# Turning gathered rows by transposing transfers in a routed mixture of experts

## The chip, the cores and the metric

One core of a Trainium2 chip runs the whole program. The metric is device time in microseconds (us) of one execution; the lower the better. TensorE (PE) multiplies matrices, VectorE (DVE) and ScalarE (ACT) work element by element, GpSimd (POOL) and SyncE (SP) mostly issue transfers (DMAs), each from a queue of its own and in program order.

## The reference, cut to what matters

A chunked attention gives rows `x` of 3072 x 512; a noisy router picks two of eight experts for each row; each expert is two products with a relu between them.

```python
N, D, E, F = (3072, 512, 8, 1024)
logits = x @ w_gate
noise_scale = np.log1p(np.exp(x @ w_noise))
noisy_logits = logits + noise_scale * noise
top2 = np.argpartition(-noisy_logits, 2, axis=1)[:, :2]
...
for e in range(E):
    for k in range(2):
        mask = top2[:, k] == e
        ...
        h = np.maximum(x[mask] @ w1[e], 0.0)
        out[mask] += top2_w[mask, k, None] * (h @ w2[e])
```

## The kernel before, in words

**Two stages.** Up to about 114 us the kernel computes the attention and the routing, and writes the rows (512 values in bf16, packed as 256 32-bit words, and eight gates) to a tensor `x_rows` in DRAM. The rest is the experts, and the change lies there.

**Buckets.** A row has two experts, so it belongs to one of 28 pairs of experts, the buckets, numbered `p`. A bucket holds up to 128 rows; what overflows goes through a small spill path. Each expert works on seven buckets, and each bucket is worked on by two experts. So expert 0 meets seven new buckets, expert 1 six, expert 2 five, and so on down to one for expert 6 and none for expert 7. `plan[e]` lists the new ones of expert `e`. `halves(e)` gives its seven buckets as a larger half of four and a smaller of three. For experts 1 and 2 the larger half is all new (expert 1: buckets 1, 9, 17, 25; the smaller half is 0, 15, 22, of which 0 is shared with expert 0); for expert 3 the new ones are exactly the larger half; from expert 4 on the larger half has been met before and the new ones are in the smaller.

**One bucket's way.** `gather(p)` (L696, GpSimd) fetches 128 rows by an indirect transfer into a tile `xl`, of which there are eight in turn. `turn(p)` needs the rows the other way round, since a product contracts over partitions: four transposes on TensorE (L705) of 128 x 128 into PSUM tile `p_t`, one copy by VectorE (L706) from there into `xTb`, which holds all 28 buckets and is never overwritten, and a copy of the gates into `meta` by ScalarE (L707). `first` (L769) multiplies `xTb` by the expert's first weights `w1t` into `ps_h`, eight blocks of the hidden width one after the other, the larger half and then the smaller; the relu (L754, L756) writes `ht`. `second` (L780) multiplies a bucket of `ht` by `w2t` into `ps_y`. The first expert of a bucket puts the result, scaled by the gate, in `acc` (L784); the second adds its own (L787), and then GpSimd scatters the bucket to the output (L788) and, for most buckets, SyncE copies its last six rows to `spart` (L795), which is read in the last expert only.

**The order.** It is written out by hand and kept on each engine. Expert 0 is special: three parts with their turns in between, a search for the spilled rows, and `turn_spill`, which makes SyncE issue six small copies to `meta` (L730). For every expert: `first`, then the gathers for the next expert (in two cases later in time, as a buffer or an index comes free), a load of weights, then the seven second products, and behind each of them one turn for the next expert:

```python
            for j, p in enumerate(order):
                second(e, p, ht, j, W2[e])
                if nxt:
                    turn(nxt.pop(0))
```

Where a tile is written by one engine or transfer and read by another, the framework puts in a wait on a semaphore. The transfers of SyncE use eight semaphores in turn, and each transfer waits until the one that used its semaphore before it has landed.

Of the kernel before, what the change touches and what calls it, by code (L numbers as in the profile page):

```python
# [12 lines left out]
F32 = mybir.dt.float32  # L13
BF16 = mybir.dt.bfloat16
# [10 lines left out]
def kernel(  # L25
# [14 lines left out]
    nc = tc.nc  # L40
# [8 lines left out]
    KP = Dm // 128  # L49
# [19 lines left out]
    XC = Dm // 2  # L69
# [29 lines left out]
    def body():  # L99
# [63 lines left out]
        for hd in range(2 * GP):  # L163
            nc.sync.dma_start(
                out=mv_nat[QW * hd + WP:QW * hd + QW].rearrange("p g e d -> p g (e d)"),
                in_=bass.AP(mem_v.tensor, mem_v.offset + hd * n_mem * D, [[2 * D, n_mem // 2], [2 * GP * n_mem * D, NG], [1, 2 * D]]))
# [518 lines left out]
        xTv = xTb.rearrange("p k (g c) -> p k g c", c=CAP)  # L685
        meta = xg.tile([128, NB, E], F32, name="meta")
# [13 lines left out]

        def turn(p, other=False):
            xl = got[p]
            p_t = psY.tile([128, KP, CAP], BF16, name="p_t2", tag="ps_y") if other else psX.tile([128, KP, CAP], BF16, name="p_t")
            for kp in range(KP):
                nc.tensor.transpose(out=p_t[:, kp, :], in_=xl[:, kp * 64:(kp + 1) * 64].bitcast(BF16), identity=identb)  # L705
            nc.vector.tensor_copy(xTv[:, :, p, :], p_t)  # L706
            nc.scalar.copy(meta[:, p, :], xl[:, XC:].bitcast(F32))  # L707
# [90 lines left out]
        plan = []  # L798
# [78 lines left out]
        for e in range(E):  # L877
# [6 lines left out]
            if e == 0:  # L884
                parts = [big[:2], big[2:], small]
                off = 0
                for x, ps in enumerate(parts):
                    for j, p in enumerate(ps):
                        turn(p, j % 2 == 1)
                    if x == 2:  # L890
                        turn_spill()
                        find_tails()
                    first(W1[e], ht, off, ps, nc.scalar if x == 0 else None, CAP if x == 2 else OWN, big if x == 2 else ())
                    off += len(ps)
                    if x == 0:
                        s_gi, s_si = find_spill()
                        gather_spill(s_gi)
                        load_w2(1)
            else:
                first(W1[e], ht, 0, big)  # L900
                first(W1[e], ht, len(big), small)
# [7 lines left out]
# [4 lines that stand above are left out]
                if e == E - 1 and j == 1:  # L913
                    for x in range(1, E // 2 - 1):
                        nc.vector.tensor_tensor(out=spart[:, 0, :], in0=spart[:, 0, :], in1=spart[:, x, :], op=Alu.add)
            if e == E - 1:
# [3 lines left out]
                    out=out_part[NB], out_offset=bass.IndirectOffsetOnAxis(ap=s_si[:, 0:1], axis=0),  # L920
                    in_=spart[:, 0, :], in_offset=None, bounds_check=N - 1, oob_is_err=False)
            while nxt:
                turn(nxt.pop(0))
# [9 lines left out]
    with tc.For_i(SPILL, end, 128) as i:  # L933
# [7 lines left out]
        for t in range(NP):  # L941
# [9 lines left out]
        xl = ld.tile([128, ROW], I32, name="xl")  # L951
        nc.gpsimd.indirect_dma_start(
            out=xl, out_offset=None, in_=xd, in_offset=bass.IndirectOffsetOnAxis(ap=gi[:, 0:1], axis=0),
# [10 lines left out]
        with tc.For_i(0, E, 1) as e:  # L964
# [17 lines left out]
            out=out, out_offset=bass.IndirectOffsetOnAxis(ap=si[:, 0:1], axis=0),  # L982
            in_=o, in_offset=None, bounds_check=N - 1, oob_is_err=False)
# [30 lines left out]
```

## Time and profile before

| | |
|---|---|
| median of 3 runs | 334.02 us (332.93 to 334.89) |
| the profiled execution | 335.33 us, span from first to last instruction 333.7 us |
| busy: TensorE, VectorE, ScalarE, GpSimd | 288.1, 169.9, 133.4, 138.6 us |
| mean granted TensorE clock | 0.957 of full speed |
| DMA packets | 58763, 42.99 MB |
| the turns: L705 on TensorE, L706 on VectorE | 112 transposes, 28 copies |

How to read it: times are microseconds from the span's start. A row of the timeline gives start, length, engine, line and the tiles as written<-read, and in brackets how long the engine sat idle before it and what ended that. Matmuls overlap in the pipeline, so the start of the next group says more about a group's cost than its own length. Rows with SPq are the queue in which SyncE issues transfers; their times are the issue and not the transfer.

### The profile page before, as it was taken

Reading aid. Unit: us, or ns where it says so; the run is one execution under the profiler, and the core shown is the slowest. Engines: PE = TensorE matmul, PEld = TensorE weight load, DVE = VectorE, ACT = ScalarE, POOL = GpSimd, SP = SyncE. Lnnn points to the kernel's source line nnn. Section 1 sums busy time; section 2 is a strip of 40 time slices with the busy share of each in tenths; the row PEclk is TensorE's granted clock in tenths of the full one; section 3 lists DMA queues with packets and bytes.
Section 4 is the critical chain, followed back from the end, with each engine's and each line's share of the span. In section 5 each row is a group of like instructions: output and inputs, shape, how many; then the busy total and the mean of one; then the engine's idle time right before and its main releaser. Section 6 shows DMA issues by size and latency. Waiting matters only on the chain.

```text
span 333.7 us, 7301 instructions
## 1 busy us (share of the span) xinstructions
PE 288.1 (86%) x3019; PEld 173.5 (52%) x3019; DVE 169.9 (51%) x343; ACT 133.4 (40%) x235; POOL 138.6 (42%) x181
## 2 busy tenths in 40 slices
PE   1697887977776377999999999999999999999990
PEld 0575675755654256554754754544544544544540
DVE  7789859849958775222322323424342433434451
ACT  7877788757433033533333332332303303202200
POOL 7877868538023472781008007007152042042152
PEclk9999999979989559999999999999999999999997
DMA  7999999999997136699407905914959624521031
GB/s 99 179 163 176 184 163 163 210 143 101 214 225 216 23 88 93 128 156 238 87 0 125 221 4 110 223 28 105 207 147 166 117 111 70 86 109 60 1 140 71
DMA packets 58763, 42.99 MB, mean 129 GB/s; under 512 B 32449, under 2 KB 52033, under 8 KB 58728
## 3 DMA queue, kind: packets, MB, share of 16 engines
q0 software_dynamic: 49808, 38.71, 77.0%
q1 hardware_dynamic: 8632, 3.74, 5.6%
q8 instruction: 24, 0.39, 0.5%
q10 hardware_dynamic: 288, 0.07, 0.1%
q14 instruction: 11, 0.09, 0.1%
HBM read 61.23 MB, written 10.66 MB: 215 GB/s over the span
## 4 chain that ended last, share of the span: by engine, by line
PE 43%; issue 24%; DVE 13%; ACT 8%; POOL 7%; DMA 3%; POOLq 0%; DVEq 0%; ACTq 0%
PE ps_h L769 16%; PE ps_y L780 14%; POOL out_dram L788 4%; ACT kd L276 3%; PE ps_o L345 3%; DMA out_dram<-acc,sidx 2%; PE ps_o L341 2%; DVE mx L313 2%; DVE xrow L358 2%; DVE sd L318 2%; DVE vg L150 2%; PE p_t L705 2%; ACT xt L371 1%; ACT P L320 1%; PE p_t L265 1%
## 5 line engine op out<-in xcount | busy, mean ns | idle before, releaser
L769 PE MATMUL ps_h<-xTb,w1t 128*128 128x512 bf16 (+5 forms) x640 | 101.4, 320 | 1.5 <-DVE xTb L706 1.5
L780 PE MATMUL ps_y<-w2t,ht 128*128 128x512 bf16 x448 | 101.4, 379 | 0.0
L769 PEld LDWEIGHTS <-w1t 128*128 128x128 bf16 x640 | 58.6, 99 | 43.9 <-DVE xTb L706 1.1
L788 POOL DMA_INDIRECT out_dram<-acc,sidx x28 | 28.1, 1004 | 126.4 <-DVE acc L787 124.1
L756 DVE TENSOR_SCALAR ht<-ps_h 128x512 bf16<-128x512 f32 (+3 forms) x68 | 38.1, 560 | 68.1 <-PE ps_h L769 63.1
L780 PEld LDWEIGHTS <-ht 128*128 128x128 bf16 x448 | 42.9, 98 | 46.7
L754 ACT ACTIVATE ht<-ps_h 128x384 bf16<-128x384 f32 (+2 forms) x76 | 38.9, 511 | 70.4 <-PE ps_h L769 66.3
L784 ACT ACTIVATE acc<-ps_y,meta 128x512 f32<-128x512 f32 x28 | 19.2, 687 | 62.6 <-PE ps_y L780 45.4
L787 DVE SCALAR_TENSOR_TENSOR acc<-ps_y,meta,acc 128x512 f32<-128x512 f32 x28 | 21.0, 750 | 34.5 <-PE ps_y L780 34.5
L696 POOL DMA_INDIRECT xl<-x_rows,gidx x28 | 30.0, 1071 | 16.8 <-PE ps_h L769 6.6
L134 POOL DMA_DIRECT2D vg<-in_v_dram x34 | 25.5, 756 | 11.4 <-DMA kg<-in_k_dram 3.7
L706 DVE COPY xTb<-p_t 128x512 bf16<-128x512 bf16 x28 | 11.6, 422 | 28.6 <-PE p_t L705 28.4
L276 ACT COPY kd<-p_t 64x768 bf16<-64x768 bf16 x32 | 25.2, 786 | 1.0 <-PE p_t L265 0.8
L265 PE MATMUL p_t<-identb,qg 128*64 128x128 bf16 x192 | 10.3, 245 | 12.0 <-DMA qg<-in_q_dram 6.6
L371 ACT COPY xt<-p_x 128x768 bf16<-128x768 bf16 x16 | 12.8, 798 | 12.0 <-PE p_x L369 11.9
L341 PE MATMUL ps_o<-memv,PT 128*128 128x260 bf16 x96 | 15.0, 296 | 2.2 <-DVE PT L332 2.0
L320 ACT ACTIVATE P<-sd 128x768 bf16<-128x768 f32 x16 | 13.5, 845 | 8.1 <-DVE sd L318 8.1
L268 ACT COPY qT<-p_t 128x768 bf16<-128x768 bf16 x16 | 12.8, 800 | 8.9 <-PE p_t L265 8.8
L358 DVE TENSOR_TENSOR xrow<-ps_o,rec 128x768 bf16<-128x768 f32 x16 | 15.3, 958 | 0.6
L313 DVE TENSOR_REDUCE mx<-ps_s 128x12 f32<-128x768 f32 x16 | 15.1, 942 | 0.5 <-PE ps_s L300 0.5
L318 DVE TENSOR_TENSOR sd<-ps_s,mx 128x768 f32<-128x768 f32 x16 | 15.2, 949 | 0.0
L345 PE MATMUL ps_o<-vg,PT 128*32 128x256 bf16 x384 | 14.9, 293 | 0.0
(150 smaller groups left out, 287.5 us busy)
## 6 DMA issues: line engine op xcount, KB each, us to landing
w1t<-in_moe_w_dram POOLq DMA_DIRECT2D x8, 1024.0 KB, 11.4
w2t<-in_moe_w_dram POOLq DMA_DIRECT2D x8, 1024.0 KB, 10.1
vg<-in_v_dram POOLq DMA_DIRECT2D x30, 168.0 KB, 10.2
qg<-in_q_dram POOLq DMA_DIRECT2D x7, 384.0 KB, 9.9
kg<-in_k_dram POOLq DMA_DIRECT2D x7, 384.0 KB, 11.3
x_rows<-xrow SPq DMA_DIRECT2D x3, 792.0 KB
x_rows<-xrow SPq DMA_DIRECT2D x2, 384.0 KB
xl<-x_rows,gidx POOLq DMA_INDIRECT x28, 6.5
```

The lines of the kernel that those rows point to most:

```text
L134: nc.gpsimd.dma_start(out=vg[p0 + j:p0 + j + nj, c:c + n, hd, :, :].rearrange("p c e d -> p c (e d)"), in_=bass.AP(v.tensor, v.offset + (g ...
L276: nc.scalar.copy(st[n]["kT"][hs, hh, :].rearrange("d (p j) -> d p j", j=SJ), st[n]["p_k"][hs].rearrange("d j p -> d p j"))
L313: nc.vector.tensor_reduce(out=mx, in_=st[n]["ps"], axis=AX, op=Alu.max)
L318: nc.vector.tensor_tensor(out=sd, in0=st[n]["ps"], in1=bc4(st[n]["mx"], CTX), op=Alu.subtract)
L345: nc.tensor.matmul(out=po[32 * r:32 * r + 32, u, :MD], lhsT=PT[:, 2 * u + e, 32 * r:32 * r + 32], rhs=vg[:, CB * half + x, :, e, :], start ...
L358: nc.vector.tensor_tensor(out=xr.rearrange("p u (h d) -> p u h d", d=D), in0=po[:, :, :MD].rearrange("p u (h d) -> p u h d", d=D), in1=rec ...
L696: nc.gpsimd.indirect_dma_start(out=xl, out_offset=None, in_=xd, in_offset=bass.IndirectOffsetOnAxis(ap=idx[:, p:p + 1], axis=0), bounds_ch ...
L754: nc.scalar.activation(out=dst, in_=src, func=Act.Relu)
L756: nc.vector.tensor_scalar(out=dst, in0=src, scalar1=0.0, scalar2=None, op0=Alu.max)
L769: nc.tensor.matmul(out=ps_h[:, o:o + w], lhsT=w1t[:, kp, f * 128:(f + 1) * 128], rhs=rhs(kp), start=(kp == 0 and i == 0), stop=(kp == KP - ...
L780: nc.tensor.matmul(out=ps_y, lhsT=ht[:, f, j * CAP:(j + 1) * CAP], rhs=w2t[:, f, :], start=(f == 0), stop=(f == FB - 1))
L788: nc.gpsimd.indirect_dma_start(out=out_part[p], out_offset=bass.IndirectOffsetOnAxis(ap=sidx[:, p:p + 1], axis=0), in_=a, in_offset=None, ...
```

## The change

For the buckets that expert 0 doesn't meet (21 of the 28), `turn` issues four transposing transfers on SyncE's queue, from `xl` straight into `xTb`, both in SBUF. The transposes of TensorE, the PSUM tile and VectorE's copy are left out for them; ScalarE's copy of the gates stays. Expert 0's seven buckets and the spilled rows are turned as before. The calls of `turn` stand where they stood.

```diff
         def turn(p, other=False):
             xl = got[p]
+            if p not in plan[0]:
+                for kp in range(KP):
+                    nc.sync.dma_start_transpose(out=xTv[:, kp, p, :], in_=xl[:, kp * 64:(kp + 1) * 64].bitcast(BF16))
+                nc.scalar.copy(meta[:, p, :], xl[:, XC:].bitcast(F32))
+                return
             p_t = psY.tile([128, KP, CAP], BF16, name="p_t2", tag="ps_y") if other else psX.tile([128, KP, CAP], BF16, name="p_t")
             for kp in range(KP):
                 nc.tensor.transpose(out=p_t[:, kp, :], in_=xl[:, kp * 64:(kp + 1) * 64].bitcast(BF16), identity=identb)
```

SyncE's order before, from the last write of `x_rows` on; the copies to `spart` are named by the buffer of `acc` that they read:

```order
L548 DMA x_rows<-xrow 128x6x8
L730 DMA meta<-xl 6x8 x6
L795 DMA spart<-acc_2650 6x512
L795 DMA spart<-acc_2657 6x512
L795 DMA spart<-acc_2651 6x512
L795 DMA spart<-acc_2663 6x512
L795 DMA spart<-acc_2658 6x512
```

And the same place now (lines below the change have moved by five):

```order
L548 DMA x_rows<-xrow 128x6x8
L735 DMA meta<-xl 6x8 x6
L705 DMA_TRANSPOSE xTb<-xl 128x128 x40
L800 DMA spart<-acc_2650 6x512
L705 DMA_TRANSPOSE xTb<-xl 128x128 x20
L800 DMA spart<-acc_2657 6x512
L800 DMA spart<-acc_2651 6x512
L705 DMA_TRANSPOSE xTb<-xl 128x128 x12
L800 DMA spart<-acc_2663 6x512
L800 DMA spart<-acc_2658 6x512
L800 DMA spart<-acc_2652 6x512
```

The first 40 are the 24 of expert 1 and 16 of expert 2's 20; the copies to `spart` now stand between transfers. With what each waits for (DMASW is a gather or another transfer of GpSimd, DMAHW one of SyncE's eight semaphores), the first nine read:

```order
L705 DMA_TRANSPOSE xTb<-xl 128x128 [waits DMASW3_49,DMASW2_49,DMASW7_49,DMASW1_49,DMAHW2_49,DMASW0_49,PE_49]
L705 DMA_TRANSPOSE xTb<-xl 128x128 [waits DMAHW3_49]
L705 DMA_TRANSPOSE xTb<-xl 128x128 [waits DMAHW4_49]
L705 DMA_TRANSPOSE xTb<-xl 128x128 [waits DMAHW5_49]
L705 DMA_TRANSPOSE xTb<-xl 128x128 [waits DMAHW6_49,DMASW1_49]
L705 DMA_TRANSPOSE xTb<-xl 128x128 [waits DMAHW7_49]
L705 DMA_TRANSPOSE xTb<-xl 128x128 [waits DMAHW0_49]
L705 DMA_TRANSPOSE xTb<-xl 128x128 [waits DMAHW1_49]
L705 DMA_TRANSPOSE xTb<-xl 128x128 [waits DMAHW2_49,DMASW2_49]
```

Before, nothing of this stood in SyncE's queue; now a bucket's first transfer waits for its gather, and every transfer for the one eight places ahead.

TensorE's order between the first two second products of expert 0, before:

```order
L780 LDWEIGHTS ht
L780 MATMUL ps_y<-w2t_164,ht 128x512
L705 LDWEIGHTS xl
L705 MATMUL p_t<-identb,xl 128x128
L705 LDWEIGHTS xl
L705 MATMUL p_t<-identb,xl 128x128
L705 LDWEIGHTS xl
L705 MATMUL p_t<-identb,xl 128x128
L705 LDWEIGHTS xl
L705 MATMUL p_t<-identb,xl 128x128
L780 LDWEIGHTS ht
L780 MATMUL ps_y<-w2t_164,ht 128x512
```

And now:

```order
L785 LDWEIGHTS ht
L785 MATMUL ps_y<-w2t_164,ht 128x512
L785 LDWEIGHTS ht
L785 MATMUL ps_y<-w2t_164,ht 128x512
L785 LDWEIGHTS ht
```

The four transposes of the turn are gone, and the products follow each other.

## The prediction

> **What bounds the kernel now.** I read the page first (busy time, the forty slices), then the chain that ended last, then a table by stretches and the waits of TensorE.
>
> The engines' busy time and two rows of the forty slices (8.34 us each):
>
> ```profile
> PE 288.1 (86%) x3019; PEld 173.5 (52%) x3019; DVE 169.9 (51%) x343; ACT 133.4 (40%) x235; POOL 138.6 (42%) x181
> ...
> PE   1697887977776377999999999999999999999990
> ...
> PEclk9999999979989559999999999999999999999997
> ```
>
> From slice 16 on (133 us) TensorE is full to the end, at full granted clock. The change lies wholly in that stretch, so TensorE's order is what it must shorten, and anything that makes TensorE wait there costs its whole length. The chain in order of time (start, length, what), from the second halves of expert 0 on; L769 is a first product (`first`), L780 a second (`second`):
>
> ```profile
> 150.83 1.73 PE ps_y L780 x8
> 152.55 12.19 PE ps_h L769 x96
> 164.74 1.73 PE ps_y L780 x8
> 166.69 1.73 PE ps_y L780 x8
> ...
> 177.94 12.19 PE ps_h L769 x96
> 190.13 1.73 PE ps_y L780 x8
> ...
> 203.11 12.11 PE ps_h L769 x64
> 215.22 1.73 PE ps_y L780 x8
> ...
> 227.97 2.60 PE ps_h L769 x12
> ```
>
> An expert takes some 25 us: 12.2 for the first product, seven second products of 1.73. Between 130 and 320 us these are TensorE's only waits, 0.9 us in all (total, times, longest):
>
> ```profile
> PE p_t L720 <- DVE xTb L706: 0.5, 1, 0.5
> PE p_t L705 <- DVE xTb L706: 0.4, 1, 0.4
> ```
>
> **What is removed.** Behind a second product that has a turn the next one starts 1.95 us later (166.69 less 164.74) and not 1.73: a turn's four transposes cost TensorE 0.22 us. The changed code leaves out 21 turns, 6 beside expert 0's second products, then 5, 4, 3, 2 and 1: 21 x 0.22 = **4.6 us**, all on the path. VectorE's copy goes too, and is worth nothing by itself:
>
> ```profile
> L706 DVE COPY xTb<-p_t 128x512 bf16<-128x512 bf16 x28 | 11.6, 422 | 28.6 <-PE p_t L705 28.4
> ```
>
> It waits for TensorE 28.6 us, never the other way in these stages except for the 0.9 above, which belong to expert 0 and stay. ScalarE's copy of the gates stays.
>
> **What is added.** SyncE issues 84 transposing transfers, four a bucket, in one queue: 24 for expert 1, 20, 16, 12, 8, 4. No such transfer stands in this trace. Nearest rows: what SyncE's transfers hold it for now (ns, min/median/max), and the gathers on GpSimd, whose starts lie 1.32 to 1.38 us apart:
>
> ```profile
> L548 SPq DMA_DIRECT2D x_rows<-xrow x6: 359/362/371, 58.8 to 111.2; - x6
> L795 SPq DMA_DIRECT2D spart<-acc x24: 663/670/743, 175.2 to 324.5; - x24
> 134.27 1.07 POOL L696 DMA_INDIRECT xl<-x_rows,gidx  x1 [6.03 <-PE ps_h L769]
> 135.65 1.02 POOL L696 DMA_INDIRECT xl<-x_rows,gidx  x1 [0.31 <-PE ps_h L769]
> 136.97 1.01 POOL L696 DMA_INDIRECT xl<-x_rows,gidx  x1 [0.30 <-PE ps_h L769]
> xl<-x_rows,gidx POOLq DMA_INDIRECT x8, 2.9
> xl<-x_rows,gidx POOLq DMA_INDIRECT x5, 10.2
> ```
>
> The last two rows are gathers' times from issue to landing, in 134 to 146 us and in 144 to 156 us, where two or three weight loads are under way. So the pace of one transfer is between 0.36 us (a plain copy of SyncE) and, as an outer bound, 2.9 us (if each held the queue until it landed). I take **1.32 us**, the gather's pace: a gather too is one instruction made into many small pieces, 128 rows of it, while SyncE's copies are few long runs. There is a second reason for a figure there: the transfers use eight semaphores in turn, and each waits for the one eight places ahead. At a landing of 2.9 us that bounds the pace at 0.36, but at 10.2 us at 1.28. I take 2.9 us from a transfer's start to its landing.
>
> [...]
>
> **The sum.** SyncE can start when expert 1's first gather has landed: 134.27 + 2.9 = 137.2. Transfer n has landed at 137.2 + 1.32(n-1) + 2.9. A first product needs its larger half (four buckets) before it begins, the other half after 4/7 of it (12.19 x 4/7 = 7.0; the rest 5.2).
>
> Expert 1. TensorE is ready at 152.55 - 6 x 0.22 = 151.2. Transfer 16 lands at 159.9: a **wait of 8.7**. After a pause TensorE's clock is lower. These rows show it (granted clock is the third figure from the right; then the chain's rows for two equal sets of 32 matmuls):
>
> ```profile
> 115.00:119.80 4.80, 1.22 (x8) 0.80 (x9) 1.61 (x10) 0.40 (x2) 3.58 (x5) 0.50 0.32 85
> 119.80:125.40 5.60, 5.59 (x33) 4.14 (x33) 5.12 (x4) 2.58 (x7) 3.83 (x3) 0.60 0.32 89
> 125.40:130.60 5.20, 4.26 (x47) 3.81 (x47) 2.56 (x11) 2.12 (x10) 1.99 (x2) 1.00 0.38 40
> 119.81 5.63 PE ps_h L769 x32
> 127.07 3.52 PE ps_h L769 x32
> ```
>
> The set behind a stretch with little work took 5.63 us at 0.60, the other 3.52: 2.1 us lost, which I add once, for this wait. Half one ends at 159.9 + 7.0 + 2.1 = 169.0. Transfer 24 lands at 170.5 (wait 1.5), half two ends at 175.7, 11.0 later than the 164.74 of the chain.
>
> Expert 2. Second products 12.1, to 187.8. Transfer 40 lands at 191.6 (**wait 3.8**); the last bucket's four stand behind one copy to spart (0.67) and land at 197.6, in time for 198.6. The first product ends at 203.8, the second products at 215.9.
>
> Expert 3. Its gathers stand on GpSimd behind the scatter of expert 1's shared bucket and a weight load:
>
> ```profile
> 174.37 0.75 DVE L787 SCALAR_TENSOR_TENSOR acc<-ps_y,meta,acc 128x512 f32<-128x512 f32 x1 [1.37 <-PE ps_y L780]
> 175.41 1.04 POOL L788 DMA_INDIRECT out_dram<-acc,sidx  x1 [24.14 <-DVE acc L787]
> 176.43 0.96 POOL L543 DMA_DIRECT2D w2t<-in_moe_w_dram  x1
> 177.70 1.08 POOL L696 DMA_INDIRECT xl<-x_rows,gidx  x1 [0.30 <-issue]
> w2t<-in_moe_w_dram POOLq DMA_DIRECT2D x8, 1024.0 KB, 10.1
> ```
>
> That bucket is the fifth second product: 175.7 + 5 x 1.73 + 0.75 + 1.04, and the gathers land after the load of 10.1: 196.2. SyncE is free just before (137.2 + 44 x 1.32 + 0.7 = 196.0). Sixteen transfers: 196.2 + 15 x 1.32 + 2.9 = 218.9 against 215.9, **wait 3.0**. One more expert (12.1 + 12.1) brings the first product of expert 4 to 243.1 where it was at 227.97: 15.1 later.
>
> From there the new halves come second and are covered. Expert 4's gathers land behind expert 2's sixth second product, two scatters and a load (203.8 + 6 x 1.73 + 0.75 + 2 x 1.04 + 10.1 = 227.1), their twelve transfers at 227.1 + 11 x 1.32 + 2.9 = 244.5, wanted at 243.1 + 7.0 = 250. Expert 5's eight stand behind copies that wait for expert 4's second products, and land about 3 us before they are wanted. Three turns left save 0.7. Together 15.1 - 0.7 = **14.4 us later**: waits of 8.7 + 1.5 + 3.8 + 3.0 and 2.1 of clock, less 4.6.
>
> Nothing else comes late. Expert 2's last three gathers wait until transfers 4, 8 and 12 have freed their buffers (154.6 for the last), and behind them on GpSimd stands a load of expert 3's weights:
>
> ```profile
> 150.43 0.84 POOL L538 DMA_DIRECT2D w1t<-in_moe_w_dram  x1
> ```
>
> It goes from 150.4 to about 156 and is wanted at 219. The copies to spart that wait in SyncE's queue are read only in the last expert.
>
> The profiled execution took 335.33 us (span 333.7), 1.3 above the median of 334.02. On it the sum gives 349.7, on the median **348.4 us**.
>
> **Rivals.** A change of 0.5% (1.7 us) is about what a measurement of this kernel tells from none. By the same walk a pace of 0.93 us gives 333, no change; that is the point that decides. A pace of 1.8 gives waits that add up to 42.7 us net, 377.
>
> 1. *A cheap transfer.* SyncE issues a transposing transfer like its other copies, 0.36 to 0.67 us. At 0.67 transfer 16 lands at 150.2, ahead of 151.2; no later one waits, and the 4.6 us are won: **329.4**, faster. For it: SyncE's own rows and its queue, idle all this time. Against it: none of its rows turns anything, and the dearer ones carry only 6 rows. Chance 0.13. [...]
>
> 2. *One at a time.* If the queue is held until a transfer has landed, the pace is 2.9: sixty transfers end at 137.2 + 174 = 311 where expert 3 began at 203.1, and with waits at experts 4 and 5 the kernel takes about **454**. For it: no transposing transfer stands in the trace, so nothing there excludes it. Against it: SyncE's copies and GpSimd's gathers leave their queues long before they land. Chance 0.05.
>
> 3. *A tie*, a pace near 0.9: waits of about 4 us take back the 4.6. Within 0.5%. Chance 0.04.
>
> **How the numbers follow.** My forecast, a pace from 0.95 to 1.8 with 1.32 likeliest, has the remaining 0.78, all of it slower. So slower 0.78 + 0.05 = 0.83, same 0.04, faster 0.13. The range runs from the tie, 333, to 378, a pace of 1.8; it leaves out rival 1, rival 2 and 0.02 between, 0.20 in all.
>
> **What would show it.** Right: SyncE's rows of L705 pitched at 1.2 to 1.4 us; TensorE's wait at L769's start for expert 1 about 9 us on xTb's transfers, two more of 3 to 4 us at experts 2 and 3, none at 5 to 7; a low clock in one slice near 160 us; second products 1.73 apart without gaps. Wrong: a pitch under 0.95 and no such waits (rival 1), a pitch that grows with the weight loads to over 1.8, waits at experts 4 to 6 too, or transfers that land long after 2.9 us, so that the last, not the pace, decides.

## The result, and the profile after

The changed kernel took 355.37 us (median of 4 runs, 350.13 to 357.6) beside 334.05 for the kernel before: a ratio of 1.0547 (95% interval 1.0426 to 1.0669), slower. Here and below a ratio is that of undisturbed runs of both kernels on one chip, so it can differ a little from the quotient of two medians. The profiled execution took 354.41 us, span 352.8, against 335.33 and 333.7: 19.1 us more span, where the sum said 14.4.

The page of the changed kernel: busy time, the slices (8.82 us each), and SyncE's DMA queue (packets, MB, share):

```profile
PE 288.5 (82%) x2935; PEld 169.9 (48%) x2935; DVE 161.2 (46%) x322; ACT 133.4 (38%) x235; POOL 138.6 (39%) x181
...
PE   1797887878773679919694899999999899999990
...
PEclk9999998989996599987999699999999999999996
...
q1 hardware_dynamic: 22072, 6.50, 9.9%
```

TensorE has 84 matmuls fewer and is as long busy as before; its mean granted clock has fallen from 0.957 to 0.938. Its row is full from 133 us on no longer: slices 17 (a tenth), 19 and 21 (counted from 0) have holes, and slices 18 and 22, behind the holes, the low clock (digits 7 and 6). Before, SyncE's queue had moved 8632 packets:

```profile
q1 hardware_dynamic: 8632, 3.74, 5.6%
```

SyncE's transfers in the changed kernel (ns, min/median/max; then its queue's timeline: start, length, count), and two steps of the chain:

```profile
L705 SPq DMA_TRANSPOSE xTb<-xl x84: 1093/1230/2133, 137.2 to 290.6; - x84
137.23 53.43 SPq L705 DMA_TRANSPOSE xTb<-xl  x40
190.76 0.73 SPq L800 DMA_DIRECT2D spart<-acc  x1
191.59 26.84 SPq L705 DMA_TRANSPOSE xTb<-xl  x20
138.51 1.21 SPq L705
139.77 1.23 SPq L705
```

A transfer holds the queue for 1.23 us and the next starts 0.05 later (139.77 less 138.51 is 1.26, 138.51 less 137.23 is 1.28), for 53 us on end. From the first start to that of the fortieth (189.18, below) it is 1.33 a transfer. Each bucket takes SyncE more than 5 us; TensorE needed 0.22.

TensorE's wait for it between 130 and 352 us (total, times, longest), and its timeline at experts 1, 2, 3, 5 and 7 (in brackets the idle time and its releaser):

```profile
PE ps_h L774 <- DMA xTb<-xl: 18.4, 6, 8.1
159.37 8.59 PE L774 MATMUL ps_h<-xTb,w1t 128*128 128x512 bf16 x33 [8.14 <-DMA xTb<-xl]
170.71 5.45 PE L774 MATMUL ps_h<-xTb,w1t 128*128 128x256 bf16 x63 [2.74 <-DMA xTb<-xl]
175.99 12.25 PE L785 MATMUL ps_y<-w2t,ht 128*128 128x512 bf16 x56
188.08 0.38 PE L774 MATMUL ps_h<-xTb,w1t 128*128 128x512 bf16 x1
191.55 0.39 PE L774 MATMUL ps_h<-xTb,w1t 128*128 128x512 bf16 x1 [3.09 <-DMA xTb<-xl]
194.92 0.59 PE L774 MATMUL ps_h<-xTb,w1t 128*128 128x512 bf16 x1 [2.98 <-DMA xTb<-xl]
195.83 13.71 PE L774 MATMUL ps_h<-xTb,w1t 128*128 128x512 bf16 x93 [0.32 <-DMA xTb<-xl]
209.37 12.25 PE L785 MATMUL ps_y<-w2t,ht 128*128 128x512 bf16 x56
221.46 12.27 PE L774 MATMUL ps_h<-xTb,w1t 128*128 128x512 bf16 x64
278.64 4.87 PE L774 MATMUL ps_h<-xTb,w1t 128*128 128x384 bf16 x29 [1.12 <-DMA xTb<-xl]
319.63 12.27 PE L774 MATMUL ps_h<-xTb,w1t 128*128 128x512 bf16 x64
```

The same places in the kernel before, in the same view:

```profile
152.39 12.35 PE L769 MATMUL ps_h<-xTb,w1t 128*128 128x512 bf16 x96
177.78 12.35 PE L769 MATMUL ps_h<-xTb,w1t 128*128 128x512 bf16 x96
202.95 12.27 PE L769 MATMUL ps_h<-xTb,w1t 128*128 128x512 bf16 x64
301.06 12.27 PE L769 MATMUL ps_h<-xTb,w1t 128*128 128x512 bf16 x64
```

With these rows the difference closes. Up to expert 3's first product (221.46 less 202.95 = 18.5 later) there are waits of 8.14 + 2.74 at expert 1 and 3.09 + 2.98 + 0.32 at expert 2, 17.3 in all. First products took 12.19 before; expert 1's now takes 175.99 - 159.37 - 2.74 = 13.9, expert 2's 209.37 - 188.08 - 6.39 = 14.9, which adds 4.4. Fifteen turns left out are worth 15 x 0.22 = 3.3. So 17.3 + 4.4 - 3.3 = 18.4. From there to expert 7 (319.63 less 301.06 = 18.6) six more turns save 1.3, a wait of 1.12 at expert 5 and some 0.3 in its pipeline take that back, and 0.5 is lost behind the last expert.

The clock in these stretches (last three figures: granted clock, DMA share, GB/s):

```profile
159.40:168.00 8.60, 8.56 (x33) 3.46 (x33) 2.13 (x4) 2.39 (x4) 1.84 (x2) 0.83 0.81 131
188.00:196.00 8.00, 1.61 (x6) 0.32 (x4) 0.00 (x0) 0.69 (x1) 4.97 (x5) 0.82 1.06 162
196.00:209.50 13.50, 13.50 (x94) 8.21 (x93) 4.44 (x7) 4.35 (x8) 0.00 (x0) 0.85 0.73 142
```

Over the two stretches behind a wait, the first row and the third, the clock averaged 0.83 and 0.85. And why expert 2's transfers landed late: the fortieth in the chain, and the load that GpSimd had issued just before:

```profile
189.18 6.60 DMA xTb<-xl
186.96 0.96 POOL L543 DMA_DIRECT2D w2t<-in_moe_w_dram  x1
```

The transfer that started at 189.18 landed 6.6 us later, at 195.78, not 2.9 later. The two ahead of it, started some 2.6 and 1.3 us earlier, were waited for until 191.55 and 194.92, some 5 and 7 us. A megabyte of weights had been issued at 186.96. At expert 1 the row of the DMA engines between 147 and 159.4 us (tenths in 40 slices of 0.31 us, and below it GpSimd's queue) reads:

```profile
DMA  9999999999999999999999999999999999996960
...
q0 software_dynamic: 1567, 2.24, 92.0%
```

The engines are full with GpSimd's loads and gathers until the last slices, and TensorE starts just behind that, at 159.37.

### The profile page after: what moved, and what is told of

It reads as the page before. It is cut to its first block, busy times and chain, and to the rows that moved or that the text cites. A ratio compares the mean times of both kernels' runs of the same rounds, so it can differ in the third digit from the quotient of the medians.

```text
span 352.8 us, 7252 instructions
## 1 busy us (share of the span) xinstructions
PE 288.5 (82%) x2935; PEld 169.9 (48%) x2935; DVE 161.2 (46%) x322; ACT 133.4 (38%) x235; POOL 138.6 (39%) x181
## 3 DMA queue, kind: packets, MB, share of 16 engines
q1 hardware_dynamic: 22072, 6.50, 9.9%
## 4 chain that ended last, share of the span: by engine, by line
PE 32%; issue 24%; SPq 14%; DVE 9%; ACT 8%; POOL 6%; DMA 5%; POOLq 0%; ACTq 0%; DVEq 0%
SPq L705 14%; PE ps_h L774 12%; PE ps_y L785 7%; POOL out_dram L793 4%; ACT kd L276 3%; PE ps_o L345 3%; PE ps_o L341 2%; DMA out_dram<-acc,sidx 2%; PE p_t L265 2%; DMA xTb<-xl 2%; ACT xt L371 2%; ACT qT L268 2%; DVE vg L150 2%; ACT P L320 1%; PE ps_s L300 1%
## 5 line engine op out<-in xcount | busy, mean ns | idle before, releaser
L774 PE MATMUL ps_h<-xTb,w1t 128*128 128x512 bf16 (+5 forms) x640 | 106.6, 328 | 19.8 <-DMA xTb<-xl 18.4
L785 PE MATMUL ps_y<-w2t,ht 128*128 128x512 bf16 x448 | 98.0, 379 | 0.0
L774 PEld LDWEIGHTS <-w1t 128*128 128x128 bf16 x640 | 59.6, 101 | 66.7 <-issue 19.3
L785 PEld LDWEIGHTS <-ht 128*128 128x128 bf16 x448 | 43.8, 98 | 51.7
L792 DVE SCALAR_TENSOR_TENSOR acc<-ps_y,meta,acc 128x512 f32<-128x512 f32 x28 | 21.0, 751 | 53.4 <-PE ps_y L785 53.4
L320 ACT ACTIVATE P<-sd 128x768 bf16<-128x768 f32 x16 | 13.5, 845 | 7.7 <-DVE sd L318 7.7
L313 DVE TENSOR_REDUCE mx<-ps_s 128x12 f32<-128x768 f32 x16 | 15.1, 943 | 1.5 <-PE ps_s L300 1.5
L265 PEld LDWEIGHTS <-qg 128*64 128x64 bf16 x192 | 7.6, 126 | 13.8 <-DMA qg<-in_q_dram 6.7
## 6 DMA issues: line engine op xcount, KB each, us to landing
w2t<-in_moe_w_dram POOLq DMA_DIRECT2D x8, 1024.0 KB, 10.2
```

Of the source, the lines that this page charges most:

```text
L265: nc.tensor.transpose(out=p_t[64 * hh:64 * hh + 64, j, :], in_=src[:, 2 * i + hh, j * D:(j + 1) * D], identity=identb)
L774: nc.tensor.matmul(out=ps_h[:, o:o + w], lhsT=w1t[:, kp, f * 128:(f + 1) * 128], rhs=rhs(kp), start=(kp == 0 and i == 0), stop=(kp == KP - ...
L785: nc.tensor.matmul(out=ps_y, lhsT=ht[:, f, j * CAP:(j + 1) * CAP], rhs=w2t[:, f, :], start=(f == 0), stop=(f == FB - 1))
```

## The experiments

**One transfer a bucket.** If the price is one of SyncE's instructions and not of bytes, a 128 x 512 transfer that turns the whole bucket costs a quarter.

```diff
-                for kp in range(KP):
-                    nc.sync.dma_start_transpose(out=xTv[:, kp, p, :], in_=xl[:, kp * 64:(kp + 1) * 64].bitcast(BF16))
+                nc.sync.dma_start_transpose(out=xTv[:, :, p, :], in_=xl[:, :XC].bitcast(BF16))
```

> The four transfers of a bucket become one, of 128 rows by 512 columns. Theory (SyncE's queue gives out one transfer after the other, and its pace per transfer decides): 21 transfers at 1.3 to 1.5 us, six of them for expert 1 done by about 137.2 + 6 x 1.4 + 4 = 150, so no wait before the first product of any expert; 4.6 us of transposes saved, about 329.5 us. Rival (the moving of the bytes decides, whoever issues it): one transfer costs as much as the four, about 5.1 us, the waits at experts 1 and 2 stay, about 350 to 355 us.

Measured: 332.71 us against 339.17 on that chip, a ratio of 0.9845 (0.9769 to 0.9921). SyncE's transfers, and its queue's packets:

```profile
L704 SPq DMA_TRANSPOSE xTb<-xl x21: 1188/1231/2109, 133.2 to 265.2; - x21
...
q1 hardware_dynamic: 20056, 6.49, 11.3%
```

Each still holds the queue for 1.23 us, with four times the data and 3.4 times the packets: (20056 - 8632)/21 = 544, against (22072 - 8632)/84 = 160. No wait on xTb's transfers is left. With a quarter of the instructions and the same bytes the slowdown is gone and the change is a gain: what was paid for is SyncE's issue, four times a bucket.

**The late experts alone.** Only experts 4 to 7's new buckets, 24 transfers, with cover for each.

```diff
-            if p not in plan[0]:
+            if p not in sum(plan[:4], []):
```

> Transfers for the six buckets of experts 4 to 7 alone; the fifteen of experts 1 to 3 are turned by TensorE as before. Theory: 24 transfers, each expert's half is wanted 7 us into its first product, so no wait; six turns of 0.22 us saved, about 332.7 us. Rival (transposing transfers slow weight loads, gathers or matmuls wherever they run): no gain or slower than 334.

Measured: 340.85 against 339.17, 1.0053 (1.0016 to 1.009). A miss: no gain. TensorE's waits, SyncE's queue and TensorE's timeline at expert 5:

```profile
PE ps_h L774 <- DMA xTb<-xl: 2.9, 3, 1.4
...
250.84 0.69 SPq L800 DMA_DIRECT2D spart<-acc  x1
251.63 6.22 SPq L705 DMA_TRANSPOSE xTb<-xl  x4
...
254.32 7.39 PE L774 MATMUL ps_h<-xTb,w1t 128*128 128x512 bf16 x34
262.84 0.32 PE L774 MATMUL ps_h<-xTb,w1t 128*128 128x384 bf16 x1 [1.13 <-DMA xTb<-xl]
264.56 6.57 PE L774 MATMUL ps_h<-xTb,w1t 128*128 128x384 bf16 x29 [1.39 <-DMA xTb<-xl]
```

Expert 5's last four transfers stand behind a copy to `spart`, which waits for expert 4's second products, and are issued from 251.63 to 257.85. The smaller half would begin some 7 us after 254.32, so the issue is in time; but TensorE waits for the last transfer until 264.56, 6.7 us after its issue ended, beside two loads of weights that GpSimd had issued at 251.35 and 253.73. That is 2.5 of the 2.9 us. Six turns of 0.22 are won, 2.9 lost: +1.6, close to the 1.7 between the medians. This is the place where the forecast counted on 3 us of cover; the landing used it up, not the issue.

**Transfers added.** TensorE and VectorE turn the buckets as before; the 84 transfers write a tile that nobody reads.

```diff
+        spare = xg.tile([128, KP, 2, CAP], BF16, name="spare")
...
-                    nc.sync.dma_start_transpose(out=xTv[:, kp, p, :], in_=xl[:, kp * 64:(kp + 1) * 64].bitcast(BF16))
-                nc.scalar.copy(meta[:, p, :], xl[:, XC:].bitcast(F32))
-                return
+                    nc.sync.dma_start_transpose(out=spare[:, kp, p % 2, :], in_=xl[:, kp * 64:(kp + 1) * 64].bitcast(BF16))
```

> All 84 transfers run, but into a spare tile that nobody reads, and TensorE and VectorE turn the buckets as before. Theory (they cost only by the wait for their data): 334 us, within 0.5%, with SyncE's pace at 1.28 us as in the changed kernel. Rival (their traffic slows the rest): 340 to 354 us, with longer matmuls, loads or gathers.

Measured: 346.83 against 339.17, 1.0262 (1.0176 to 1.0348). A miss, and an instructive one. Waits of TensorE and ScalarE, SyncE's queue, TensorE's timeline (this kernel's L784 is `second`, L788 the write of `acc`):

```profile
PE ps_y L784 <- ACT acc L788: 5.9, 1, 5.9
ACT acc L788 <- DMA spart<-acc: 9.9, 3, 7.8
...
135.14 61.62 SPq L706 DMA_TRANSPOSE spare<-xl  x40
...
197.60 32.66 SPq L706 DMA_TRANSPOSE spare<-xl  x20
230.31 1.41 SPq L799 DMA_DIRECT2D spart<-acc  x2
...
233.16 5.58 PE L784 MATMUL ps_y<-w2t,ht 128*128 128x512 bf16 x16 [5.94 <-ACT acc L788]
```

Two copies to `spart` stand behind 60 transfers until 230.31. They read buffers of `acc` that ScalarE wants to write again; ScalarE waits, `ps_y` isn't emptied, and TensorE stands for 5.9 us. So what stands behind the transfers in SyncE's queue can cost too, and the prediction had passed it as harmless. Part of the delay is this kernel's own: its spare tile holds two buckets, and SyncE waits 15.1 us in 14 places for an earlier transfer into it, so that 40 transfers take 61.6 us and not 53.4. The 5.9 us are most of the 7.7 between the medians; where the rest goes is not shown, and for it the rival (traffic) stands. In the changed kernel itself TensorE has no such wait: there it comes later than the copies.

**The turns left out.** What the turns cost, by themselves; this kernel leaves out 21 buckets' values.

```diff
-                for kp in range(KP):
-                    nc.sync.dma_start_transpose(out=xTv[:, kp, p, :], in_=xl[:, kp * 64:(kp + 1) * 64].bitcast(BF16))
+                nc.vector.memset(xTv[:, :, p, :], 0.0)
```

> The 21 turns of experts 1 to 7 are left out: VectorE writes zeros into xTb in place of its copy, TensorE transposes nothing for them, no transfer is issued (so the output lacks these buckets' values). Theory: 4.6 us less, 21 turns of 0.22 us, about 329.5 us. Rival (the transposes were filled into gaps): 333 to 334 us.

Measured: 334.21 against 339.17, 0.9875 (0.9795 to 0.9955), which on 339.17 is 4.2 us (1.5 to 7.0). The 4.6 of the sum lies well within. It is also the ceiling of this change: one transfer a bucket reaches it.

**Landing beside loads.** The next four ran on another chip, whose kernel before took 333.82. First the changed kernel once more, as a base.

> The changed kernel once more, beside the others on one chip. Theory: 15 to 20 us slower than before on the same chip, waits of about 8 and 3 us at expert 1 and about 6 us at expert 2, SyncE's pace 1.28 us. Rival (the first measurement caught a disturbed chip): under 10 us slower.

Measured: 353.66, 1.0592 (1.054 to 1.0645), with 18.4 us of waits in six places as in the first run.

Then the load of expert 3's second weights is issued ahead of expert 1's second products, instead of behind them, where it met transfers 37 to 40.

```diff
             if e + 2 < E:
                 load_w1(e + 2)
+            if e == 1:
+                load_w2(e + 2)
...
-            if e + 2 < E:
+            if e + 2 < E and e != 1:
                 load_w2(e + 2)
```

> The changed kernel, with the load of expert 3's second weights issued before expert 1's second products and not behind the scatter among them, so that it no longer moves while transfers 37 to 40 land. Theory (their landing of 3.5 to 6.6 us, against 2.9 when little else moves, is the load's doing): the waits at expert 2's first product fall from 6.4 to about 3 us, 3 to 4 us faster than the changed kernel on the same chip. Rival (a transposing transfer takes that long to land by itself): no difference. SyncE's pace stays at 1.28 us either way, though more of expert 2's transfers run beside a load; if the load set the pace it would rise.

Measured: 350.38, 1.0477 (1.0438 to 1.0515): 3.3 us less than the base, and the intervals don't meet. TensorE's waits and expert 2's first product:

```profile
PE ps_h L774 <- DMA xTb<-xl: 14.6, 7, 8.2
192.53 12.35 PE L774 MATMUL ps_h<-xTb,w1t 128*128 128x512 bf16 x96
```

Expert 2's first product starts at once and runs its 12.35 without a break. The load now lies beside expert 1's last transfers, and expert 1's waits are 12.9 us of the 14.6, where the base on this chip has 9.9. With the pitch unchanged (the first forty take 53.4 us, 53.3 in the base), the place of one load moved the waits: late landing beside a load is a cost of its own.

**Two transfers a bucket**, each 128 x 256.

```diff
-                for kp in range(KP):
-                    nc.sync.dma_start_transpose(out=xTv[:, kp, p, :], in_=xl[:, kp * 64:(kp + 1) * 64].bitcast(BF16))
+                for kp in range(0, KP, 2):
+                    nc.sync.dma_start_transpose(out=xTv[:, kp:kp + 2, p, :], in_=xl[:, kp * 64:(kp + 2) * 64].bitcast(BF16))
```

> Two transfers of 128 x 256 for a bucket and not four. Theory (a price per transfer, 1.28 us whatever its size): 2.6 us a bucket, below the 3.8 us (four at 0.95) at which waits begin to take back the gain; transfer 8 lands at about 137.2 + 7 x 1.28 + 4 = 150, so no wait of over 0.5 us, 4 to 5 us faster than before on the same chip. Rival (a price by size): 2.5 us each, the waits of the changed kernel, 15 to 20 us slower than before.

Measured: 1.0118 (1.0072 to 1.0165), slower, a miss. Waits, and the chain's last step ahead of expert 1's second half:

```profile
PE ps_h L774 <- DMA xTb<-xl: 4.3, 3, 3.1
149.09 13.23 DMA xTb<-xl
```

SyncE started expert 1's last transfer at 149.09 and it landed 13.2 us later, beside the two loads issued at 138.41 and 139.21. By the pitch alone there would have been no wait.

**One transfer a bucket, and five of expert 0's buckets too.**

```diff
-            if p not in plan[0]:
+            if p not in halves(0)[0][:2]:
```

The transfer itself is that of the first experiment.

> One transfer a bucket, and five of expert 0's seven buckets too (all but the first two, for which TensorE has nothing else to do). Theory: their gathers land 3 to 8 us before they are wanted, so that 5 turns and the waits for VectorE's copies between them go, 1 to 2.5 us more than one transfer a bucket for experts 1 to 7 gains: 6 to 7 us faster than before on the same chip. Rival (in this stretch the landing is on the path): no gain over that, or a loss of 1 to 3 us.

Measured: 0.9954 (0.9878 to 1.0031), which rests on two of twelve runs and doesn't tell it from no change. Its profiled execution, of 337.53 us, is not one of the two (334.3 and 330.57), so these waits don't explain the ratio:

```profile
PE ps_h L773 <- DMA xTb<-xl: 8.2, 2, 4.5
144.12 18.96 DMA xTb<-xl
```

In it a transfer landed after 19 us beside loads, and TensorE waited for it. This left open whether one transfer a bucket keeps its gain on every chip, for in the first experiment something had given it time: ScalarE stood for 2.5 us in expert 0's second products, and TensorE with it.

**The loads behind the gathers.** The loads of expert 2's weights, which those transfers meet, go behind expert 2's gathers; with one and with two transfers a bucket, and beside them one a bucket as it was.

```diff
+            if e == 1:
+                load_w1(2)
+                load_w2(2)
...
-            if e + 2 < E:
+            if 0 < e < E - 2:
                 load_w1(e + 2)
...
-            if e + 2 < E:
+            if 0 < e < E - 2:
                 load_w2(e + 2)
```

> One transfer a bucket once more, for the same chip as the two kernels below. In a kernel with one transfer a bucket and five more for expert 0, expert 1's last transfer started at 144 us and landed only at 163, beside two weight loads. Theory (issue is cheap now, but a transfer beside a weight load lands 8 to 19 us late, so expert 1 may still wait): 0 to 8 us of waits on xTb, time between 4.6 us faster and 3 us slower than before. Rival (only the pace counts): 4.6 us faster, no wait.

> One transfer a bucket, and the loads of expert 2's two weights stand on GpSimd behind the gathers for expert 2, which wait for buffers that expert 1's first transfers free: so nothing big moves while expert 1's transfers land. Theory: they land within 3 to 5 us, no wait at expert 1, 4 to 5 us faster than before. Rival (landing is slow by itself, or the loads now come late): a wait at expert 1 as with one transfer a bucket, or one at expert 2's weights.

> Two transfers a bucket with the same order of loads. With loads beside them this was 4 us slower than before, with waits of 4.3 us on xTb. Theory: eight transfers for expert 1's larger half are issued by 137 + 8 x 1.28 = 147.5 and land by 151, just when they are wanted; waits under 1 us, 3 to 5 us faster than before. Rival (the pace of 2.6 us a bucket is itself too slow): waits of 3 to 4 us stay.

Measured: one a bucket 0.9863 (0.9803 to 0.9924); with the loads behind, 0.9959 (0.9924 to 0.9993); two a bucket with the loads behind, 0.9987 (0.9947 to 1.0027), where it had been 1.0118 on the other chip. None of the three waits for xTb's transfers: for two a bucket the wait of 4.3 us is gone. The trace's marks of each landing put this down to the loads: the eighth transfer, the last of expert 1's larger half, took 2.3 us (145.26 to 147.60), and 8.7 in the run beside the loads (143.81 to 152.54). TensorE came to it at 158.97; without the 6.3 us of other waits shown next that would have been 152.7, still late enough. But the moved loads gained nothing over one a bucket as it was. What TensorE waits for there (two a bucket, loads behind):

```profile
PE ps_y L785 <- DVE ht L761: 6.3, 2, 4.8
```

and the chain of one a bucket in the same place (an execution of 337.67 us, longer than the kernel's others):

```profile
141.12 3.43 another core or an unknown queue
```

A relu of ScalarE stands for 3.4 us, for something that the profile doesn't name, and the products with it. On two chips every kernel that was profiled had this pause (waits of 3.2 to 6.3 us in these products), the one without transposing transfers too; in the traces of the kernel before and of the changed kernel, taken on other chips, it isn't there. The kernel before took 339.17 and 338.85 us on these two and 333 to 334 on the others, which would fit a pause there too, but no profile of it was taken on them. With the loads behind the gathers the waits were longer (5.8 and 6.3 us against 3.5). Its cause stays open.

**One transfer a bucket, a third time**, to see it without that pause.

> One 128x512 transfer a bucket, as in the two runs before (0.9845 and 0.9863). In both, ScalarE stood still for 2.5 to 3.5 us in expert 0's second products, which gives the transfers that much more time; on the chip of two_per_bucket no such pause was seen, and there transfers that landed 13 to 19 us after their start were waited for. Theory (the price is the transfers' number, and landing beside the loads is a second, smaller one): with the pause again 0.985 and no wait on xTb; without it expert 1's first product waits 1 to 5 us for transfers that started by 143 and land 8 to 19 us later, and the ratio is 0.99 to 1.005. Rival (landing plays no part once there is one transfer a bucket): no wait and 0.985 in both cases.

Measured: 328.05 us against 332.84, 0.9887 (0.9829 to 0.9946), on another chip and without the pause. The waits, and two steps of the chain:

```profile
PE ps_h L773 <- DMA xTb<-xl: 0.5, 1, 0.5
...
133.88 3.21 DMA xTb<-xl
142.64 12.41 DMA xTb<-xl
```

The first transfer, ahead of the two loads of weights issued at 138.43 and 139.23, landed 3.2 us after its start; the one that started at 142.64, beside them, landed 12.4 later and was waited for 0.5 us, less than the 1 to 5 expected. So the gain doesn't hang on the pause, and this version beats both kernels: 4.8 us between the medians, 3.8 (1.8 to 5.7) by the ratio; the turns' 4.6 lie within.

## Why the prediction was right, and where not

**The pace: right in size, its reason not.** It was taken as 1.32 us from the gather; the rows show 1.26 to 1.28 between neighbours and 1.33 over the first forty. It is the price of an instruction: one transfer a bucket has the same 1.23 us for four times the data. That the gather's figure was so near is largely luck. The reason given was many small pieces against SyncE's few long runs. But SyncE's last copy to `x_rows`, 128x6x8, is 768 pieces by its shape (784 packets in the profile before) and held the queue 0.36 us, and 544 packets of a transposing transfer hold it no longer than 160. The second reason, the wait for the transfer eight places ahead, is not among SyncE's waits. What in a transposing instruction takes 1.23 us no run shows. Rivals 1 and 3 needed a pace under 0.95, rival 2 one of 2.9.

**What is removed: right.** 4.6 us was the sum, 4.2 measured by itself, and 0.22 a turn closes the account above.

**Expert 1: right.** 8.7 + 1.5 was said, 8.14 + 2.74 came. The step said that TensorE waits for transfer 16 before it begins. The rows of expert 2 show single matmuls with a wait between them: the first matmul needs the first of the four blocks of the contraction for four buckets, which takes transfer 13, and the next three need 14, 15 and 16. So transfer 16 still bounds the fourth matmul, and the slip is worth three matmuls at most, 0.7 us. In the run transfer 13, started at 153.56, was waited for until 159.37, when the load had left the DMA engines: 5.8 us and not 2.9. Transfer 16 started at 157.34 and would be due at 160.2 by the 2.9 us alone, where the sum had 159.9; from 159.37 on TensorE ran without a break. So at expert 1 the pace set the wait, and the late landing cost some half a us.

**The landing: the step that was mis-sized.** 2.9 us was taken, the median of gathers in a quiet stretch: the text puts both of its rows beside two or three loads, but six of the eight gathers of the first were issued by 140.92, before the loads of 141.94 and 142.74. The row of 10.2 beside it, of gathers among loads, was used for a bound of the pace and not for the landing. The 2.9 holds without loads (3.2 us in the last experiment) and not beside them: about 5, 7 and 6.6 for three transfers of expert 2. That made its wait 6.4 where 3.8 was said. The experiment that moved the load showed it: with the load elsewhere that wait is gone. Late landing also held buffers: expert 2's last gather started at 159.62, not 154.6. And the load said to go from 150.4 to about 156 took 12.5 us from issue to landing in the profile before; neither came onto the path. The text had named late landings as a way to be wrong.

**Expert 3: the wait of 3.0 didn't come.** SyncE ended its second run of transfers at 191.59 + 26.84 = 218.4, close to what the sum had (the last start at 216.0, landed by 218.9), but TensorE, later from expert 2, got there only at 221.46 and not at 215.9. The lateness was paid one expert earlier.

**The clock: 4.4 us lost and not 2.1.** It was added once; there were two such waits, with a clock of 0.83 and 0.85 behind them. Expert 1's first product lost 13.9 - 12.2 = 1.7 us. At expert 2 the 93 matmuls from 195.83 on took 13.5 us to 209.37, where 12.19 less three of 0.22 is 11.5: 2.0 lost. Each is near the 2.1 of the sum; the count was wrong. The other 0.7 of the 4.4 goes to the three single matmuls between waits.

**Later experts.** No wait at 4, 6 and 7 as said; at expert 5, where 3 us of cover were counted, 1.12 of wait. SyncE had issued expert 5's last transfer by 272.95, and it was waited for until 278.64, beside two loads issued at 266.87 and 269.25: late landing again. With the late experts alone the wait there was 2.5, in the same way.

**The copies to `spart`: wrong as said, without effect on the time.** They were called harmless as their result is read last; they also free `acc`, as the experiment with transfers added showed (5.9 us of TensorE).

Together, against 14.4: expert 1 +0.7, expert 2 +2.6, expert 3 -3.0, expert 5 +1.1, clock +2.3, the rest of expert 5 and the tail +0.8: 18.9 of the 19.1.

## What to carry to other kernels

Work that leaves a full engine for a queue can be bound by that queue's issue: count the instructions and price each, not the bytes (1.23 us here for 32 KB as for 128). Here one instruction instead of four a bucket turned 5% slower into 1.1 to 1.6% faster. Then ask what else the transfers fly beside, since the landing (here up to 19 us after the start) and not the issue ends a wait, and what stands behind them in the queue, with the buffers that it frees (5.9 us of TensorE in one run).

## What the runs showed of the hardware

A transposing transfer from SBUF to SBUF held SyncE's queue for a median of 1.23 us whether it turned 128 x 128 (160 packets) or 128 x 512 (544 packets).

From its start to its landing it took 3.2 us (128 x 512) ahead of the loads; beside loads of weights it took 5 to 7 us (128 x 128), 13.2 (128 x 256) and 12.4 (128 x 512; 19 in the execution of 337.53 us), though it is 32 to 128 KB against their megabyte. The larger ones landed later than 128 x 128, but not in the order of their size (13.2 and 12.4), and what makes them late no run shows: a transfer also stood behind others of its own queue that had not landed, so size and place are not told apart.
